# A DiT block on one core: transposing bf16 activations on TensorE as 4-byte pairs of neighbouring values

## The chip, the cores and the metric

The kernel is one block of a diffusion transformer (DiT) and runs on one core of one Trainium2 chip. The metric is the device time of one execution in microseconds (us), the median of several runs. Most runs of one kernel on one chip lie within about 0.3% of each other.

Names used below: PE is TensorE's matmul stream and PEld its weight loads, DVE is VectorE, ACT is ScalarE, POOL is GpSimd. SBUF is the on-chip memory that holds the operands, PSUM the one that matmuls write to. A "k-tile" is one of the 9 pieces of 128 features into which the model width of 1152 is cut. LN1 and LN2 are the two LayerNorms.

## The reference, cut to what matters

```python
B, N, D = 2, 256, 1152            # 512 tokens in 4 tiles of 128; 9 k-tiles
shift_a, scale_a, gate_a, shift_m, scale_m, gate_m = ...   # silu(c) @ w_mod
h = layernorm(x) * (1 + scale_a) + shift_a
q, k, v = (h @ wqkv) ...                                   # 2 heads of 576
attn = softmax(q @ k.T * Dh ** -0.5)
x = x + gate_a * ((attn @ v) @ wo)
h2 = layernorm(x) * (1 + scale_m) + shift_m
out = x + gate_m * (gelu(h2 @ w_fc1) @ w_fc2)              # width 4 * D
```

The kernel's matmuls contract over partitions (the 128 rows of the on-chip memories). So the outputs of LN1, softmax and LN2, which have tokens on partitions, must be transposed before the next matmul. The kernel does it on TensorE: the data is the stationary operand, an identity is the moving one, the result lands in PSUM, and VectorE or ScalarE carries it on to SBUF, applying the LayerNorm's scale on the way.

## The kernel before: the parts that matter

LN1. `ps16(bank, c, n)` is a bf16 view of a PSUM bank; there are 8 banks.

```python
XB = [(4, 5, 6), (6, 4, 5)]
def xn_T(t):                      # 9 transposes for each token tile
    b = t // 2
    for kt in range(KT):
        tr(ps16(XB[b][kt // 4], (kt % 4) * 256 + (t % 2) * 128, 128), XN[:, t, kt * 128:(kt + 1) * 128], IDENT)
# ... cut: k-tiles 0 to 4 are scaled from PSUM (hk), k-tiles 5 to 8 are copied (xnT_cp)
for kt in range(KC):
    hk(kt, 0, "act" if kt in (2, 4) else "dve")
```

LN2: k-tiles 0 to 3 go to bank 7 and 4 to 8 to bank 6. In the first two token tiles VectorE scales 0 to 3 and ScalarE 4 to 8.

```python
def xn2_T(t):
    slot = [ps16(7, kt * 128, 128) if kt < 4 else ps16(6, (kt - 4) * 128, 128) for kt in range(KT)]
    for kt in range(KT):
        tr(slot[kt], xn2[:, kt * 128:(kt + 1) * 128], IDENT)
    for kt in range(KT):
        if kt < (4 if t < 2 else 6):
            dve(335, lambda ...: e.tensor_scalar(out=dst, in0=o, scalar1=s1, scalar2=s2, ...), ..., "h2T_%d_%d" % (t, kt))
        else:
            act(440, lambda ...: e.activation(out=dst, in_=o, func=ACTF.Identity, scale=s1, bias=s2), ..., "h2T_%d_%d" % (t, kt))
```

The kernel schedules itself: a list scheduler puts the units of work of VectorE and ScalarE in an order, from dependences that a tracker records. The tracker's rule for PSUM:

```python
for b in reg.banks():
    if eng == "pe":
        # ... cut: a PE write waits for every earlier reader of the whole bank
    else:
        for u in self.bank_pe[b]:
            self._add_dep(ins, u.instrs[-1])       # a reader waits for the last transpose of the tile that wrote to the bank
        for o in self.bank_other[b]:
            if o.unit.eng != eng:
                self._add_dep(ins, o)              # and for each earlier reader of the bank on ANOTHER engine
            # ... cut: readers on the same engine
```

The rule is needed. The Trainium skill, "PSUM — Partial Sum Buffer", section "PSUM bank collisions raise a hardware error", says that no two of TensorE, ScalarE and VectorE may be in one bank and 32-partition quadrant at once, reads against reads included, and that software has to keep them apart.

Of the kernel before, what the change touches and what calls it, by code (L numbers as in the profile page):

```python
# [492 lines left out]
BF16 = mybir.dt.bfloat16  # L493
F32 = mybir.dt.float32
ALU = mybir.AluOpType
ACTF = mybir.ActivationFunctionType
AX = mybir.AxisListType

P = 128
NTOK = 512  # L500
D = 1152
KT = 9
# [5 lines left out]
CH = 384  # L508
NCH = 3
F0 = 8  # L510
KC = 5
# [3 lines left out]
def c_mm(n):  # L515
    return max(n / 2.4 + 2.5, 27.0)
# [26 lines left out]
def build_kernel(nc, x, c, wqkv, wo, w_mod, w_fc1, w_fc2, out):  # L543
    S = Sched()
# [4 lines left out]
    with (  # L549
        nc.sbuf_tensor("arena", [P, ARENA_BYTES // 2], BF16) as arena,  # L550
        nc.psum_tensor("psum", [P, 4096], F32) as psum,
        nc.Block() as block,
    ):
        def sb(off, nbytes, dt=BF16):
            assert off % 4 == 0 and off + nbytes <= ARENA_BYTES, (off, nbytes)
            v = arena[:, off // 2:(off + nbytes) // 2]
            if dt == F32:
                v = v.bitcast(F32)
            return v
# [22 lines left out]
        def misc(nbytes):  # L582
            o = mo[0]
            mo[0] += (nbytes + 3) // 4 * 4
            assert mo[0] <= ARENA_BYTES
            return o
# [36 lines left out]
        IDENT = sb(misc(256), 256)  # L623
        ONES = sb(misc(256), 256)
        CSB = sb(misc(256), 256)
        TH = sb(misc(72), 72, F32)
# [23 lines left out]
        outv = out.rearrange("b (p t) d -> b p t d", t=2)  # L650
        wqkv_v = wqkv.rearrange("(k p) f -> p k f", p=P)
        wmod_v = w_mod.rearrange("(k p) f -> p k f", p=P)
        wo_v = wo.rearrange("(k p) f -> p k f", p=P)
        wfc1_v = w_fc1.rearrange("(k p) f -> p k f", p=P)
        wfc2_v = w_fc2.rearrange("(k p) f -> p k f", p=P)

        def dma(dst, src, nbytes, name, is_out=False, eng="sp", run=4096):
            eff = 1.0 if run >= 4096 else (1.08 if run >= 2304 else (1.15 if run >= 1536 else (1.3 if run >= 1024 else 1.42)))
            return S.op(eng, 500.0 if eng == "sp" else 150.0, lambda e: e.dma_start(dst, src), reads=[src], writes=[dst],  # L659
                        name=name, dma_bytes=nbytes * eff, is_out=is_out)  # L660

        def dve(cost, fn, reads, writes, name):
# [14 lines left out]
        def mm(o, l, r, st, sp, **kw):  # L677
            S.instr(lambda e: e.matmul(o, lhsT=l, rhs=r, start=st, stop=sp, **kw), reads=[l, r], writes=[o])  # L678

        def tr(o, i_, idn):  # L680
            S.instr(lambda e: e.transpose(o, i_, idn), reads=[i_, idn], writes=[o])  # L681
# [5 lines left out]
        for (ka, kb) in ((0, KC), (KC, KT)):  # L687
            w = (kb - ka) * P
            for k0 in range(0, KT, 3):
                dma(WSC[:, k0:k0 + 3, ka * P:kb * P], wmod_v[:, k0:k0 + 3, D + ka * P:D + kb * P], 3 * P * w * 2,  # L690
                    "ld_sc%d_%d" % (ka, k0), run=w * 2)
            for kt in range(ka, kb):
                dma(WK[:, kt, :], wqkv_v[:, kt, D:2 * D], P * D * 2, "ld_wk%d" % kt, run=2304)
        for k0 in range(0, KT, 3):
            dma(WSH[:, k0:k0 + 3, :], wmod_v[:, k0:k0 + 3, 0:D], 3 * P * D * 2, "ld_sh%d" % k0, run=2304)

        def wfc1_load(q):
            dma(WFC1[q % 4], wfc1_v[:, :, q * 512:(q + 1) * 512], D * 512 * 2, "ld_wfc1_%d" % q, run=1024)

# [3 lines left out]
             reads=[ONES], writes=[IDENT], name="ident")  # L703

        S.op("pool", 100, lambda e: e.memset(NHALF, -0.5), writes=[NHALF], name="nhalf")

# [44 lines left out]
        def xn_T(t):  # L751
            b = t // 2
            S.unit("pe", KT * c_mm(128), "xnT_%d" % t)
            for kt in range(KT):
                tr(ps16(XB[b][kt // 4], (kt % 4) * 256 + (t % 2) * 128, 128), XN[:, t, kt * 128:(kt + 1) * 128], IDENT)

        def xn_T_copy(b, k0, k1, eng):
            src = ps16(XB[b][k0 // 4], (k0 % 4) * 256, (k1 - k0) * 256).rearrange("p (k t) -> p k t", k=k1 - k0)
            copy_on(eng, HX[:, k0:k1, b * 256:(b + 1) * 256], src, (k1 - k0) * 256, True, "xnT_cp%d_%d" % (b, k0))

# [5 lines left out]
        def mod_kt(W, kt, col0, name, fs=(0, 9)):  # L766
            S.unit("pe", (fs[1] - fs[0]) * 27.0, name)
            for f in range(*fs):
                mm(ps32(7, col0 + f * 2, 2), W[:, kt, f * 128:(f + 1) * 128], ST[:, kt:18:9], kt == 0 and f == fs[0], kt == KT - 1,
                   skip_group_check=True)  # L770
# [6 lines left out]
        def hk(kt, b, eng="dve"):  # L777
            dst, s1 = HK[:, kt, b * 256:(b + 1) * 256], SC1A[:, kt * 2 + b:kt * 2 + b + 1]
            src = ps16(XB[b][kt // 4], (kt % 4) * 256, 256) if kt < KC else HX[:, kt, b * 256:(b + 1) * 256]
            if eng == "act":  # L780
                act(c_act(256, 1), lambda e: e.activation(out=dst, in_=src, func=ACTF.Copy, scale=s1), [src, s1], [dst], "hk_%d_%d" % (kt, b))
                return
            dve(256 if kt < KC else 200, lambda e: e.tensor_scalar(out=dst, in0=src, scalar1=s1, scalar2=None, op0=ALU.mult),  # L783
                [src, s1], [dst], "hk_%d_%d" % (kt, b))
# [38 lines left out]
        for kt in range(KC):  # L823
            hk(kt, 0, "act" if kt in (2, 4) else "dve")
        xn_T_copy(0, 8, 9, "act")
        xn_T_copy(0, 5, 8, "act")
        for kt in range(KC):
            for i in range(4):
                k_pair((kt,), i, 0)
            if kt == 1:  # L830
                xn_T(2)
            if kt == 2:
                xn_T(3)
                xn_T_copy(1, 8, 9, "act")
                xn_T_copy(1, 5, 8, "act")
        for kt in range(KC):
# [10 lines left out]
        for kt in range(KT):  # L847
            dma(WQ[:, kt, :], wqkv_v[:, kt, 0:D], P * D * 2, "ld_wq%d" % kt, run=2304)
        for kt in range(KC, KT - 2):
# [25 lines left out]
        for kt in range(KT):  # L875
            mod_kt(WSH, kt, 18, "sh_%d" % kt)
        dma(WV, wqkv_v[:, :, 2 * D:3 * D], D * D * 2, "ld_wv", run=2304)
        for k0 in range(0, KT, 3):
# [3 lines left out]
        for kt in range(KT):  # L882
            for b in range(2):
# [5 lines left out]
                else:  # L889
# [9 lines left out]
                    "sc1a_0", "hk_0_0", "xn_2", "hk_1_0", "xn_3", "hk_3_0", "z4a", "hk_0_1", "hk_1_1", "hk_3_1", "hk_4_1", "sc1a_5"],  # L899
            "act": ["ld_c", "c_tanh", "sq_ln1_0", "sum_ln1_0", "sq_ln1_3", "sum_ln1_3", "xnT_cp0_8", "xnT_cp0_5", "hk_2_0", "hk_4_0",  # L900
                    "hk_2_1", "xnT_cp1_8", "xnT_cp1_5"],
        }
# [27 lines left out]
        def pt_transposes(b, h):  # L930
            idx = b * 2 + h
            bank = s_bank[(b, h)]
            S.unit("pe", 4 * c_mm(128), "PT_%d_%d" % (b, h))
            for kjt in range(2):
                for jq in range(2):
                    tr(ps16(bank, kjt * 256 + jq * 128, 128), PP[idx][:, jq, kjt * 128:(kjt + 1) * 128], IDENT)
            copy_on("dve" if b == 0 else "act", PTS[idx].rearrange("p j k -> p (j k)"), ps16(bank, 0, 512), 512, True, "PT_ev%d" % idx)

# [3 lines left out]
        def v_proj(t, ci):  # L942
            bank = v_banks[v_rr[0] % 3]
            v_rr[0] += 1
            S.unit("pe", KT * c_mm(CH), "v_%d_%d" % (t, ci))
            o = ps32(bank, 0, CH)
            for kt in range(KT):
                mm(o, HX[:, kt, t * 128:(t + 1) * 128], WV[:, kt, ci * CH:(ci + 1) * CH], kt == 0, kt == KT - 1)
            copy_on("act" if v_rr[0] % 2 else "dve", V[:, t, ci * CH:(ci + 1) * CH], o, CH, False, "v_ev%d_%d" % (t, ci))
# [23 lines left out]
        def rows_T():  # L973
            for j, bank in ((0, 3), (1, 4)):
                S.unit("pe", 9 * 30.0 + 100.0, "rowsT%d" % j)
                for r in range(3):
                    for i3 in range(3):
                        ft = r * 3 + i3
                        tr(ps16(bank, ft * 2, 2), ROWS[32 * j:32 * j + 2, r, i3 * 128:(i3 + 1) * 128], IDENT[32 * j:32 * j + 2, 32 * j:32 * j + 2])
            a, b_ = ps16(3, 0, 18), ps16(4, 0, 18)  # L980
            dve(170, lambda e: e.tensor_copy(SHM, a), [a], [SHM], "shm")
            dve(170, lambda e: e.tensor_scalar(out=SC1M, in0=b_, scalar1=1.0, scalar2=None, op0=ALU.add), [b_], [SC1M], "sc1m")
# [52 lines left out]
        def xn2_T(t):  # L1035
            b = t // 2
            xn2 = XN2[t]
            S.unit("pe", KT * c_mm(128), "xn2T_%d" % t)
            slot = [ps16(7, kt * 128, 128) if kt < 4 else ps16(6, (kt - 4) * 128, 128) for kt in range(KT)]
            for kt in range(KT):  # L1040
                tr(slot[kt], xn2[:, kt * 128:(kt + 1) * 128], IDENT)
            for kt in range(KT):
# [153 lines left out]
```

## Time and profile before

| | before |
|---|---|
| time, median of 4 runs | 249.73 us (249.42 to 249.81) |
| profiled span | 247.4 us |
| PE busy | 241.7 us, 98% |
| first K matmul to the second-half modulation matmuls (LN1 stretch) | 6.66 us |
| from there to the first LN2 transpose | 78.30 us |
| first LN2 transpose to the end of the fourth LN2 tile (LN2 stretch) | 12.62 us |
| first LN2 transpose to the last matmul | 147.38 us |

The last four rows are differences of matmul start times in the trace (of the last matmul, its end). Since PE is busy nearly all the time, such a table of PE's own milestones says which stage a change moved.

From the profile page of the kernel before: the span, PE's row, and the chain of waits that ended last, by engine.

```profile
span 247.4 us, 4146 instructions
...
PE 241.7 (98%) x1827; PEld 149.5 (60%) x1827; DVE 69.9 (28%) x179; ACT 63.8 (26%) x129; POOL 19.6 (8%) x33
...
PE 94%; ACT 2%; DMA 2%; DVE 1%; issue 0%
```

PE bounds the kernel. Before, from its groups of instructions by line (L681 is the transpose helper, L1049 and L1046 are the LN2 scalings, L783 the LN1 scalings). The columns are busy us and mean ns of one, then idle time before and what ended it:

```profile
L681 PE MATMUL psum<-arena 128*128 128x128 bf16 (+2 forms) x107 | 7.8, 209 | 0.9 <-DMA arena<-in_c_dram 0.7
L1049 ACT ACTIVATE arena<-psum,arena 128x128 bf16<-128x128 bf16 x16 | 6.1, 460 | 3.2 <-PE psum L681 2.5
L1046 DVE TENSOR_SCALAR arena<-psum,arena 128x128 bf16<-128x128 bf16 x20 | 5.5, 338 | 2.0 <-PE psum L681 1.8
L783 DVE TENSOR_SCALAR arena<-psum,arena 128x256 bf16<-128x256 bf16 x7 | 2.4, 349 | 2.7 <-PE psum L681 1.4
```

The 209 ns is the length of one record; records overlap. Successive transposes start 55.9 ns apart, and that spacing is what they cost PE.

Before, timeline of the first LN2 tile's scalings and the second tile's transposes (start us, us, engine, line, count, idle before):

```profile
97.68 1.16 ACT L1049 ACTIVATE arena<-psum,arena 128x128 bf16<-128x128 bf16 x3 [1.94 <-PE psum L681]
97.68 0.60 DVE L1046 TENSOR_SCALAR arena<-psum,arena 128x128 bf16<-128x128 bf16 x2
...
98.78 1.35 ACT L1033 ACTIVATE arena<-arena 128x1152 bf16<-128x1152 f32 x1
...
100.03 0.79 ACT L1049 ACTIVATE arena<-psum,arena 128x128 bf16<-128x128 bf16 x2
...
100.24 0.37 PEld L681 LDWEIGHTS psum<-arena 128*128 128x128 bf16 x4
...
100.87 0.28 PEld L681 LDWEIGHTS psum<-arena 128*128 128x128 bf16 x5 [0.26 <-ACT arena L1049]
```

ScalarE does three scalings, then the next tile's normalisation (L1033, 1.35 us), then its last two, ending at about 100.82. Meanwhile PE does the second tile's first four transposes, into bank 7, which VectorE has left. Only the five for bank 6 wait, 0.26 us of idle weight load. (Elsewhere in this text a gap on PE is the time between two matmul starts beyond their usual spacing, which comes to 0.25 us here; the brackets in the views give idle time, which is often shorter.)

### The profile page before, as it was taken

What the parts mean: (1) busy time and instruction counts of PE and PEld (TensorE: products, weight loads), DVE (VectorE), ACT (ScalarE), POOL (GpSimd) and SP (SyncE); (2) the same over time, 40 slices, a digit from 0 to 9 for tenths busy, and PEclk for the clock granted to TensorE, in tenths of its full rate; (3) what the DMA queues carried; (4) which work ended last, traced back from release to release, by engine and by line L of the source; (5) the groups of instructions that cost most, each with busy time, mean ns of one, the idle gap of its engine ahead of it and who ended that gap; (6) DMA issues with size and microseconds to landing.
All of it is one profiled execution on the core that took longest, in us unless ns stands there. A gap on an engine that the chain in (4) does not pass through costs nothing.

```text
span 247.4 us, 4146 instructions
## 1 busy us (share of the span) xinstructions
PE 241.7 (98%) x1827; PEld 149.5 (60%) x1827; DVE 69.9 (28%) x179; ACT 63.8 (26%) x129; POOL 19.6 (8%) x33
## 2 busy tenths in 40 slices
PE   6999999999999999999999999999999999999995
PEld 2589954566656766798544444444566666666674
DVE  3742440555322679950000000000012222111112
ACT  4730340344301404984333222332000000000000
POOL 1300000000013167500000000000000000000000
PEclk9999999999999999999999999999999999999999
DMA  6999989999999999999953660000000000000000
GB/s 240 372 375 393 390 299 414 426 423 420 409 385 332 309 364 391 392 386 383 358 156 138 191 191 3 0 0 0 3 16 16 19 16 16 16 19 21 27 19 17
DMA packets 27644, 51.59 MB, mean 209 GB/s; under 512 B 1511, under 2 KB 15591, under 8 KB 26475
## 3 DMA queue, kind: packets, MB, share of 16 engines
q1 hardware_dynamic: 27216, 50.14, 56.0%
q0 software_dynamic: 384, 1.19, 1.5%
q8 instruction: 14, 0.23, 0.4%
q14 instruction: 3, 0.02, 0.0%
q10 hardware_dynamic: 27, 0.00, 0.0%
HBM read 50.14 MB, written 1.19 MB: 208 GB/s over the span
## 4 chain that ended last, share of the span: by engine, by line
PE 94%; ACT 2%; DMA 2%; DVE 1%; issue 0%
PE psum L678 92%; PE psum L681 2%; DMA arena<-in_x_dram 2%; ACT arena L1049 1%; ACT arena L1033 1%; ACT arena L731 1%; ACT arena L730 1%; DVE arena L744 0%; DVE arena L783 0%; DVE arena L1139 0%; DVE arena L732 0%; DVE arena L1140 0%; DVE arena L774 0%; DVE arena L734 0%
## 5 line engine op out<-in xcount | busy, mean ns | idle before, releaser
L678 PE MATMUL psum<-arena 128*128 128x384 bf16 (+7 forms) x1720 | 237.7, 305 | 1.8 <-POOL arena L701 1.4
L678 PEld LDWEIGHTS psum<-arena 128*128 128x128 bf16 (+1 forms) x1720 | 143.8, 97 | 91.0 <-issue 3.1
L1139 DVE TENSOR_TENSOR arena<-psum,arena 128x384 f32<-128x384 f32 (+3 forms) x14 | 7.0, 501 | 119.2 <-PE psum L678 119.2
L1059 ACT ACTIVATE arena<-psum 128x512 bf16<-128x512 f32 (+1 forms) x44 | 22.5, 522 | 42.6 <-PE psum L678 42.6
L673 ACT ACTIVATE arena<-psum 128x512 bf16<-128x512 f32 (+7 forms) x29 | 15.4, 553 | 36.2 <-PE psum L678 33.8
L675 DVE CAST arena<-psum 128x512 bf16<-128x512 f32 (+4 forms) x23 | 14.0, 621 | 32.1 <-PE psum L678 32.0
L1028 POOL TENSOR_TENSOR arena<-arena 128x384 f32<-128x384 f32 x12 | 11.0, 913 | 11.2 <-DVE arena L1027 10.0
L722 DVE BATCH_NORM_STATS2 arena<-arena 128x6 f32<-128x384 f32 (+1 forms) x18 | 9.5, 548 | 0.8 <-DMA arena<-in_x_dram 0.7
L681 PE MATMUL psum<-arena 128*128 128x128 bf16 (+2 forms) x107 | 7.8, 209 | 0.9 <-DMA arena<-in_c_dram 0.7
L681 PEld LDWEIGHTS psum<-arena 128*128 128x128 bf16 (+2 forms) x107 | 6.3, 97 | 3.7 <-DMA arena<-in_c_dram 1.6
L1033 ACT ACTIVATE arena<-arena 128x1152 bf16<-128x1152 f32 x4 | 5.4, 1353 | 9.5 <-DVE arena L1032 9.5
L1027 DVE TENSOR_TENSOR arena<-psum,arena 128x384 f32<-128x384 f32 x12 | 6.6, 548 | 3.2 <-PE psum L678 2.6
L1140 DVE TENSOR_TENSOR arena<-arena 128x384 bf16<-128x384 f32 (+3 forms) x14 | 7.0, 501 | 0.5
L1049 ACT ACTIVATE arena<-psum,arena 128x128 bf16<-128x128 bf16 x16 | 6.1, 460 | 3.2 <-PE psum L681 2.5
L659 POOL DMA_DIRECT2D dit_scratch<-arena x2 | 1.2, 629 | 61.3 <-DVE arena L675 61.3
L1046 DVE TENSOR_SCALAR arena<-psum,arena 128x128 bf16<-128x128 bf16 x20 | 5.5, 338 | 2.0 <-PE psum L681 1.8
L924 ACT ACTIVATE arena<-psum,arena 128x256 bf16<-128x256 f32 x8 | 3.7, 471 | 6.9 <-PE psum L678 5.4
L726 POOL TENSOR_TENSOR arena<-arena 128x1 f32<-128x1 f32 x6 | 3.3, 553 | 8.7 <-DVE arena L725 8.7
L887 ACT ACTIVATE arena<-arena 128x256 bf16<-128x256 bf16 x6 | 2.5, 496 | 4.3 <-DVE arena L881 4.3
L920 DVE TENSOR_REDUCE arena<-psum 128x2 f32<-128x512 f32 x4 | 2.8, 690 | 1.5 <-PE psum L678 1.5
L783 DVE TENSOR_SCALAR arena<-psum,arena 128x256 bf16<-128x256 bf16 x7 | 2.4, 349 | 2.7 <-PE psum L681 1.4
L928 DVE TENSOR_TENSOR arena<-arena 128x512 bf16<-128x512 bf16 x4 | 2.8, 688 | 0.1
(37 smaller groups left out, 30.9 us busy)
## 6 DMA issues: line engine op xcount, KB each, us to landing
arena<-in_w_mod_dram SPq DMA_DIRECT2D x3, 3456.0 KB, 25.9
arena<-in_w_fc_dram SPq DMA_DIRECT2D x9, 1152.0 KB, 8.6
arena<-in_w_fc_dram SPq DMA_DIRECT2D x4, 2592.0 KB, 20.7
arena<-in_wqkv_dram SPq DMA_DIRECT2D x18, 288.0 KB, 10.0
arena<-in_w_mod_dram SPq DMA_DIRECT2D x3, 864.0 KB, 13.1
arena<-in_wqkv_dram SPq DMA_DIRECT2D x1, 2592.0 KB, 10.0
arena<-in_wo_dram SPq DMA_DIRECT2D x1, 2592.0 KB, 39.7
arena<-in_w_mod_dram SPq DMA_DIRECT2D x3, 480.0 KB, 6.8
```

Source lines behind the costliest of these rows:

```text
L673: act(c_act(n), lambda e: e.activation(out=dst, in_=src, func=ACTF.Copy), [src], [dst], name)
L675: dve(c_dve_psum16(n) if psum16 else c_dve_psum32(n), lambda e: e.tensor_copy(dst, src), [src], [dst], name)
L678: S.instr(lambda e: e.matmul(o, lhsT=l, rhs=r, start=st, stop=sp, **kw), reads=[l, r], writes=[o])
L681: S.instr(lambda e: e.transpose(o, i_, idn), reads=[i_, idn], writes=[o])
L722: dve(550, lambda e, s=s, o=o: e.bn_stats(out=o, in_=s), [s], [o], "bn_%s_%d" % (tag, ci))
L1027: dve(550, lambda e, o=o, ga=ga, x1c=x1c: e.tensor_tensor(out=x1c, in0=o, in1=ga, op=ALU.mult), [o, ga], [x1c], "wo_t1_%d_%d" % (t, ci))
L1028: S.op("pool", 930, lambda e, xs=xs, x1c=x1c: e.tensor_tensor(out=x1c, in0=x1c, in1=xs, op=ALU.add), reads=[x1c, xs], writes=[x1c], name=" ...
L1033: act(1344, lambda e: e.activation(out=xn2, in_=x1, func=ACTF.Identity, scale=rs, bias=nm), [x1, rs, nm], [xn2], "xn2_%d" % t)
L1049: act(440, lambda e, o=o, dst=dst, s1=s1, s2=s2: e.activation(out=dst, in_=o, func=ACTF.Identity, scale=s1, bias=s2), [o, s1, s2], [dst], ...
L1059: act(c_act(ntok), lambda e: e.activation(out=dst, in_=o, func=ACTF.Gelu_apprx_tanh), [o], [dst], "gelu_%d_%d" % (f, tok0))
L1139: dve(c_dve_psum32(w), lambda e, o=o, gm=gm, t1=t1: e.tensor_tensor(out=t1, in0=o, in1=gm, op=ALU.mult), [o, gm], [t1], "fc2_t1_%d_%d" % ( ...
L1140: dve(c_dve_32(w), lambda e, t1=t1, x1c=x1c, ost=ost: e.tensor_tensor(out=ost, in0=t1, in1=x1c, op=ALU.add), [t1, x1c], [ost], "fc2_out_%d ...
```

## The change

A 128x256 block of bf16 is a 128x128 block of 4-byte words, each holding two neighbouring features. One 4-byte transpose then does the work of two: row p of the result holds features 2p and 2p+1 of the pair of k-tiles, alternating. Since 9 is odd, the first 128 features keep a 2-byte transpose of their own. The rest follows from the interleaving: weight rows are loaded in a permuted order to match, the engines that empty PSUM read every second bf16, and modulation columns and V tokens are taken with a step of two. The intent is fewer PE instructions, 5 transposes for 9 in each LayerNorm tile and 2 for 4 in each softmax tile. Core of the diff, cuts marked:

```diff
+        def tr4(o, i_):
+            o4, w0 = o.bitcast(F32R), int(i_.offset) % (ARENA_BYTES // 2) // 2
+            S.instr(lambda e: e.transpose(o4, words[:, w0:w0 + P], IDENT4W), reads=[i_, IDENT4], writes=[o])
 # ... cut: weight loads with permuted rows, fcols() = every second column
         def xn_T(t):
             b = t // 2
-            for kt in range(KT):
-                tr(ps16(XB[b][kt // 4], (kt % 4) * 256 + (t % 2) * 128, 128), XN[:, t, kt * 128:(kt + 1) * 128], IDENT)
+            tr(ps16(XB[b][2], (t % 2) * 128, 128), XN[:, t, 0:P], IDENT)
+            for g in range(4):
+                tr4(ps32(XB[b][g // 2], (g % 2) * 256 + (t % 2) * 128, 128), XN[:, t, P + 256 * g:P + 256 * (g + 1)])
 # ... cut: xn_src() = every second bf16 of PSUM; one copy of 1024 elements for two of 256 and 768
         def pt_transposes(b, h):
-            for kjt in range(2):
-                for jq in range(2):
-                    tr(ps16(bank, kjt * 256 + jq * 128, 128), PP[idx][:, jq, kjt * 128:(kjt + 1) * 128], IDENT)
+            for jq in range(2):
+                tr4(ps32(bank, jq * 128, 128), PP[idx][:, jq, :])
 # ... cut: V tokens with a step of two
         def xn2_T(t):
-            slot = [ps16(7, kt * 128, 128) if kt < 4 else ps16(6, (kt - 4) * 128, 128) for kt in range(KT)]
-            for kt in range(KT):
-                tr(slot[kt], xn2[:, kt * 128:(kt + 1) * 128], IDENT)
+            slot = [ps16(6, 512, 128)]
+            tr(slot[0], xn2[:, 0:P], IDENT)
+            for g in range(4):
+                bank, c0 = (7, g * 128) if g < 2 else (6, (g - 2) * 128)
+                tr4(ps32(bank, c0, 128), xn2[:, P + 256 * g:P + 256 * (g + 1)])
+                v = ps16(bank, 2 * c0, 256).rearrange("p (t i) -> p i t", i=2)
+                slot += [v[:, 0, :], v[:, 1, :]]
```

In LN2 each 4-byte result holds a pair of k-tiles, so bank 7 now holds k-tiles 1 to 4 and bank 6 holds 5 to 8 and, behind them, k-tile 0. The split of work between the engines (VectorE 0 to 3, ScalarE 4 to 8) is left as it was.

## The prediction

> **What bounds the kernel.** The profile page has PE busy for 241.7 of 247.4 us; the chain of waits lies on PE for 94% of the span, and from 15.8 us on it leaves PE only at the second-LayerNorm (LN2) transposes (97.7 to 100.8 us, ScalarE) and at the end. Starts in the trace are even: 128x512 matmuls every 215.8 ns, 384 every 162.5, 256 every 109.2, two-column modulation matmuls every 26.7, transposes every 55.9. PE time removed is time saved, unless something else is just behind PE.
>
> **What the change does on PE.** 88 transposes cost 88 x 55.9 = 4.92 us. After: 8 bf16 ones and 40 four-byte ones, each still one weight load and one matmul. No trace here times a four-byte one; call it p. The PE change is 40p - 80 x 55.9 ns: -2.2 us at p = 56, zero at p = 112. The data is the stationary operand. The Trainium skill, "TensorE: Matmul & The Clock Gate", "Weight-path perf modes", excludes FP32 from fast weight load, and its "LDWEIGHTS" section gives columns / 1.2, so 107 ns for 128. I expect the load to set p: 70 to 115 ns, central estimate 90, and PE work to fall by about 0.9 us.
>
> **What stands just behind PE.**
> - LN1: the second-half modulation weights land at 19.05 us; the matmuls needing them start at about 19.3. At most 0.3 us of LN1's saving can show. The new placement puts k-tiles 1 to 4 in one bank, used alternately by VectorE and ScalarE: the third tile's transposes wait for ScalarE's scaling of k-tile 4, 0.3 to 0.6 us of new stall near 14 us. It also separates ScalarE's copy from k-tile 4, removing two stalls before 18.5 us (0.06, 0.13 us). Net 0 to 0.2 us gained.
> - Softmax: four tiles on the chain: 4 x (224 - 2p), 0.2 us gained.
> - LN2: 4 x (503 - 56 - 4p), 0.35 us gross, but the second tile already waits for ScalarE (0.25 us) and arriving earlier only lengthens that. Net 0 to 0.2.
>
> **Added work elsewhere.** VectorE reads every second bf16 of PSUM. 512-element copies took 424 ns (bf16) and 690 ns (fp32), so I estimate half rate for strided reads: +133 ns on a 256-element scaling (349 to about 480), +67 on a 128-element one (338 to about 405), +266 on softmax copies. Mostly off the chain; perhaps 0.2 us of waiting in LN2. ScalarE: one 1024-element copy near 1.05 us replaces 384 + 805 ns. Modulation and V weight loads now step by two elements; I expect the 26.7 ns pace to hold. If it doubled, 144 loads would cost 3.8 us: the largest risk. Weight bytes and run lengths are unchanged; 20 more DMA issues should not be felt.
>
> **Prediction.** 249.3 us, 8 in 10 between 247.9 and 251.8. Faster by over 2%: 2%; within 2%: 92%; slower by over 2%: 6%.
>
> **What would show it.** Four-byte transposes starting 70 to 115 ns apart; strided VectorE scalings near 480 and 405 ns; a gap inside the third LN1 tile near 14 us waiting for ScalarE; two-column matmuls still 26.7 ns apart; second-half modulation matmuls beginning at most 0.3 us earlier; LN2 gaps of 0.2 to 0.6 us at the second or fourth tile.
>
> **What would make it wrong.** p near 56 with no new LN2 waits: about 248.5. p of 160 or more (load and matmul not overlapping): 251 to 253. Strided weight loads slower than the 26.7 ns pace: up to 4 us worse. Strided reads stalling the first feed-forward tiles by over 0.5 us.

## More of the kernel before

Before, windows of the trace (start:end, length, then busy us of each engine), for the LN1 stretch, what lies between, and the LN2 stretch:

```profile
core 0: us, PE busy (x) PEld busy (x) DVE busy (x) ACT busy (x) POOL busy (x), PEclk, DMA share, GB/s
12.02:18.68 6.66, 6.66 (x68) 5.74 (x69) 3.11 (x9) 2.29 (x5) 0.00 (x0) 1.00 1.08 377
18.68:96.98 78.30, 78.30 (x715) 51.08 (x713) 34.74 (x85) 21.01 (x48) 11.00 (x15) 1.00 1.02 381
96.98:109.60 12.62, 12.53 (x118) 9.93 (x117) 9.84 (x30) 11.34 (x23) 5.47 (x8) 1.00 1.05 392
```

In the LN2 stretch ScalarE is busy 11.3 of 12.6 us and VectorE 9.8: these two have little slack there.

## The result, and the profile after

The kernel after took 250.69 us (median of 4 runs, 250.44 to 250.94) against 249.73 before in the same rounds. The ratio is 1.0042, 95% interval 1.0027 to 1.0056: "the same" at 2%, but a small loss for certain. A ratio here is the mean time of one kernel's fast runs over the mean of the other's in the same rounds, so it is not quite the ratio of the medians quoted beside it.

Work was taken off PE, as the page shows, and yet the span grew:

```profile
span 249.1 us, 4079 instructions
...
PE 240.2 (96%) x1777; PEld 148.3 (60%) x1787; DVE 71.5 (29%) x179; ACT 63.8 (26%) x127; POOL 19.9 (8%) x34
...
PE 91%; DMA 3%; DVE 2%; ACT 1%; SPq 1%; issue 1%
```

After, groups by line (L705 is the 4-byte transpose; L1091, L1088 and L822 answer to L1049, L1046 and L783):

```profile
L1091 ACT ACTIVATE arena<-psum,arena 128x128 bf16<-128x128 bf16 x16 | 6.1, 461 | 4.8 <-PE psum L701 4.8
L1088 DVE TENSOR_SCALAR arena<-psum,arena 128x128 bf16<-128x128 bf16 x20 | 6.5, 390 | 2.5 <-PE psum L705 2.5
...
L705 PE MATMUL psum<-ident,words 128*128 128x128 f32 x40 | 6.0, 261 | 0.4 <-DVE arena L909 0.4
...
L822 DVE TENSOR_SCALAR arena<-psum,arena 128x256 bf16<-128x256 bf16 x7 | 2.9, 443 | 2.4 <-PE psum L705 1.7
```

The means of L1088 and L822 mix strided reads with the plain reads of k-tile 0. Strided alone they take about 402 ns (338 before) and 475 to 484 ns (349 before). ScalarE's take 461 (460): no cost there.

After, windows for the same three stretches:

```profile
core 0: us, PE busy (x) PEld busy (x) DVE busy (x) ACT busy (x) POOL busy (x), PEclk, DMA share, GB/s
...
12.41:19.21 6.80, 6.43 (x61) 5.66 (x62) 3.68 (x9) 2.34 (x4) 0.00 (x0) 1.00 1.08 378
19.21:97.17 77.96, 77.78 (x703) 50.89 (x704) 35.28 (x85) 21.02 (x48) 10.99 (x15) 1.00 1.03 383
97.17:111.30 14.13, 12.47 (x103) 9.27 (x100) 10.01 (x30) 11.47 (x23) 5.47 (x8) 1.00 1.03 385
```

| stage, in PE's milestones | before | after | difference |
|---|---|---|---|
| start to the first K matmul | 12.02 | 12.41 | +0.39 |
| LN1 stretch | 6.66 | 6.80 | +0.14 |
| up to LN2 (softmax lies here) | 78.30 | 77.97 | -0.33 |
| first LN2 transpose to the last matmul | 147.38 | 148.90 | +1.52 |
| sum, to the last matmul | 244.36 | 246.07 | +1.71 |

The first row looks like chance: the first K matmul waits for modulation weights, and over all 13 traces of whole kernels it starts between 11.66 and 12.54 us with no relation to the form of LN1 (two-byte LN1: 12.02, 12.05, 12.35, 12.39, 12.54; four-byte: 11.66 to 12.54). Without it the trace has +1.33 us, and the timed runs +0.96. So the stage sums are good to some 0.4 us, and the story is the last row: LN2 lost 1.5 us.

After, the timeline that answers to the one of before:

```profile
97.85 0.66 DVE L1088 TENSOR_SCALAR arena<-psum,arena 128x128 bf16<-128x128 bf16 x2
...
98.28 0.81 ACT L1091 ACTIVATE arena<-psum,arena 128x128 bf16<-128x128 bf16 x2 [2.35 <-PE psum L701]
...
98.86 0.72 DVE L1088 TENSOR_SCALAR arena<-psum,arena 128x128 bf16<-128x128 bf16 x2
98.98 1.34 ACT L1071 ACTIVATE arena<-arena 128x1152 bf16<-128x1152 f32 x1
...
100.23 1.14 ACT L1091 ACTIVATE arena<-psum,arena 128x128 bf16<-128x128 bf16 x3
...
101.48 0.10 PEld L708 LDWEIGHTS psum<-arena 128*128 128x128 bf16 x1 [1.22 <-DVE arena L754]
101.51 0.22 PE L708 MATMUL psum<-arena 128*128 128x128 bf16 x1 [0.86 <-DVE arena L1065]
```

ScalarE no longer starts together with VectorE. VectorE's first scaling, k-tile 0 in bank 6, runs from 97.85 to 98.18; ScalarE's semaphore event passes at 98.22 and its first scaling, in the same bank, starts at 98.28. The same is seen in the second tile (VectorE's k-tile 0 ends at 102.79, ScalarE starts at 102.89). Having started late, ScalarE fits only two scalings ahead of the normalisation, so three remain and the last ends at 101.37 (before: 100.82). And since k-tile 0's transpose, the first of the tile, goes into bank 6, the whole second tile waits for it: PE's semaphore event is at 101.41 and the weight load at 101.48.

The bracket names VectorE's L1065 as the releaser, the multiplication of a later tile's attention output by its gate. It neither writes what the transposes read nor reads their banks; it merely ended at about the same time. The PE gap is 1.03 us long. Two more follow: 0.64 us in all inside the first feed-forward tile (0.10 us until VectorE's k-tile 3 is scaled, then 0.54 us until k-tile 4 is, which lies in VectorE's bank 7 and which the scheduler now puts fourth of ScalarE's five), and 0.60 us before the fourth tile's transposes. Before, LN2's gaps summed to 0.31 us. So the waits grew by 1.96 us while four tiles saved 4 x 0.12 = 0.47 us.

Near 14 us, in the third LN1 tile, the stall that was predicted from the same rule (L820 is ScalarE's scaling of k-tile 4, L909 an idle-time memset):

```profile
14.20 0.34 PE L705 MATMUL psum<-ident,words 128*128 128x128 f32 x2
14.29 0.47 ACT L820 ACTIVATE arena<-psum,arena 128x256 bf16<-128x256 bf16 x1 [0.55 <-DVE arena L822]
...
14.88 0.14 PEld L705 LDWEIGHTS psum<-ident,words 128*128 128x128 f32 x1 [0.48 <-DVE arena L909]
```

PE stops after two 4-byte transposes, until ScalarE has left the bank: about 0.53 us. Here too the bracket names an innocent instruction.

### The profile page after: what moved, and what is told of

It is laid out like the page before. It is cut to its first block, busy times and chain, and to the rows that moved or that the text cites. A ratio compares the mean times of both kernels' runs of the same rounds, so it can differ in the third digit from the quotient of the medians.

```text
span 249.1 us, 4079 instructions
## 1 busy us (share of the span) xinstructions
PE 240.2 (96%) x1777; PEld 148.3 (60%) x1787; DVE 71.5 (29%) x179; ACT 63.8 (26%) x127; POOL 19.9 (8%) x34
## 4 chain that ended last, share of the span: by engine, by line
PE 91%; DMA 3%; DVE 2%; ACT 1%; SPq 1%; issue 1%
PE psum L701 90%; DMA arena<-in_w_mod_dram 3%; ACT arena L1091 1%; PE psum L705 1%; SPq L666 1%; DVE arena L1065 1%; DVE arena L1088 0%; PE psum L708 0%; DVE arena L753 0%; DVE arena L1070 0%; ACT arena L1101 0%; DVE arena L822 0%; DVE arena L909 0%; DVE arena L1181 0%; DVE arena L1182 0%
## 5 line engine op out<-in xcount | busy, mean ns | idle before, releaser
L1101 ACT ACTIVATE arena<-psum 128x512 bf16<-128x512 f32 (+1 forms) x44 | 22.5, 522 | 42.6 <-PE psum L701 42.6
L696 ACT ACTIVATE arena<-psum 128x512 bf16<-128x512 f32 (+6 forms) x27 | 15.3, 582 | 35.5 <-PE psum L701 33.4
L1065 DVE TENSOR_TENSOR arena<-psum,arena 128x384 f32<-128x384 f32 x12 | 6.6, 548 | 3.2 <-PE psum L701 3.0
L1091 ACT ACTIVATE arena<-psum,arena 128x128 bf16<-128x128 bf16 x16 | 6.1, 461 | 4.8 <-PE psum L701 4.8
L1088 DVE TENSOR_SCALAR arena<-psum,arena 128x128 bf16<-128x128 bf16 x20 | 6.5, 390 | 2.5 <-PE psum L705 2.5
L705 PE MATMUL psum<-ident,words 128*128 128x128 f32 x40 | 6.0, 261 | 0.4 <-DVE arena L909 0.4
L705 PEld LDWEIGHTS psum<-ident,words 128*128 128x128 f32 x40 | 4.4, 141 | 0.9 <-DVE arena L909 0.5
L708 PE MATMUL psum<-arena 2*128 2x2 bf16 (+2 forms) x27 | 2.5, 179 | 2.5 <-DVE arena L1065 0.9
L708 PEld LDWEIGHTS psum<-arena 2*128 2x128 bf16 (+2 forms) x27 | 1.3, 93 | 5.0 <-DMA arena<-in_c_dram 1.7
L822 DVE TENSOR_SCALAR arena<-psum,arena 128x256 bf16<-128x256 bf16 x7 | 2.9, 443 | 2.4 <-PE psum L705 1.7
```

What stands on the lines that cost most here:

```text
L696: act(c_act(n), lambda e: e.activation(out=dst, in_=src, func=ACTF.Copy), [src], [dst], name)
L705: S.instr(lambda e: e.transpose(o4, words[:, w0:w0 + P], IDENT4W), reads=[i_, IDENT4], writes=[o])
L1065: dve(550, lambda e, o=o, ga=ga, x1c=x1c: e.tensor_tensor(out=x1c, in0=o, in1=ga, op=ALU.mult), [o, ga], [x1c], "wo_t1_%d_%d" % (t, ci))
L1088: dve(335, lambda e, o=o, dst=dst, s1=s1, s2=s2: e.tensor_scalar(out=dst, in0=o, scalar1=s1, scalar2=s2, op0=ALU.mult, op1=ALU.add), [o, s ...
L1091: act(440, lambda e, o=o, dst=dst, s1=s1, s2=s2: e.activation(out=dst, in_=o, func=ACTF.Identity, scale=s1, bias=s2), [o, s1, s2], [dst], ...
L1101: act(c_act(ntok), lambda e: e.activation(out=dst, in_=o, func=ACTF.Gelu_apprx_tanh), [o], [dst], "gelu_%d_%d" % (f, tok0))
```

## The experiments

The main theory: LN2's new PSUM places make two engines take turns in one bank, and this alone is the loss. Rivals: the slower strided reads of VectorE; the LN1 stall; a higher cost of 4-byte transposes in context; another order of work that the scheduler picked. Twelve runs were made of eleven kernels, in four groups: experiments 1 to 4; 5, 6, 7 and 8; 9, h1_all_banks and g1_again; and h2_act_order. Each group has runs of the kernel before on its own chip (experiment 8 was run once, for its trace only). Groups 1 and 2 ran on the same chip.

### 1. LN2 put back, the rest of the change kept (e1_ln2_bf16)

```diff
-            slot = [ps16(6, 512, 128)]
-            # ... one two-byte and four 4-byte transposes
+            slot = [ps16(7, kt * 128, 128) if kt < 4 else ps16(6, (kt - 4) * 128, 128) for kt in range(KT)]
+            for kt in range(KT):
+                tr(slot[kt], xn2[:, fcols(kt)], IDENT)
```

> The changed kernel with only its LN2 transposes put back to two-byte ones in the old PSUM places (weights stay permuted; the transposes read every second column). Theory A (the loss is the new PSUM placement in LN2: k-tile 0 lies in the bank that ScalarE drains, k-tile 4 in VectorE's, so engines and the next tile's transposes wait): in the changed kernel's trace LN2 lost 1.5 us against before, so about 249.2 us here, 0.2 to 0.8 us below the kernel before, and the gaps of 1.03, 0.54 and 0.60 us on PE between 100 and 111 us go back to the 0.25 and 0.06 us of before. Rival B (the loss is in LN1 or in later weights): about 250.5 us and the LN2 gaps unchanged in size.

Measured: 248.99 us, ratio 0.9974 (0.9959 to 0.9989), now faster than before. LN2's gaps are those of the kernel before and the LN2 stretch is 12.62 us. So the loss sits in LN2's part of the change.

### 2. LN1 put back, the rest kept (e3_ln1_plain)

```diff
-            tr(ps16(XB[b][2], (t % 2) * 128, 128), XN[:, t, 0:P], IDENT)
-            # ... 4-byte transposes, strided sources, permuted weight rows
+            for kt in range(KT):
+                tr(ps16(XB[b][kt // 4], (kt % 4) * 256 + (t % 2) * 128, 128), XN[:, t, kt * 128:(kt + 1) * 128], IDENT)
```

> The changed kernel with LN1 wholly as before (two-byte transposes, old PSUM places, unpermuted rows of the qkv and modulation weights); softmax and LN2 four-byte. In the changed kernel's trace the first 60 us lost 0.5 us, of which 0.4 came before the first K matmul because a modulation weight landed 0.76 us later. Theory D (that lateness is chance or belongs to one trace, the LN1 part itself is worth nothing): within 0.2 us of the changed kernel, 250.5 to 250.8. Rival E (LN1's part costs 0.5 us in every run): 250.2 us, and the weight lands at 10.3 us again.

Measured: 250.77 us, ratio 1.0043 (1.0029 to 1.0056), the same as the kernel after (1.0042). The LN1 stretch is 6.66 us, as before, against 6.80. The LN1 part is worth nothing measurable as written: its transposes are cheaper and its stall takes that back.

### 3. The kernel before, with LN2's PSUM places alone changed (f1_before_banks)

```diff
-            slot = [ps16(7, kt * 128, 128) if kt < 4 else ps16(6, (kt - 4) * 128, 128) for kt in range(KT)]
+            slot = [ps16(6, 512, 128) if kt == 0 else ps16(7, (kt - 1) * 128, 128) if kt < 5 else ps16(6, (kt - 5) * 128, 128) for kt in range(KT)]
```

No 4-byte transpose and no strided read is in this kernel; only addresses in PSUM differ.

> The kernel before with nothing changed but the LN2 PSUM places: k-tile 0 in the bank of k-tiles 5 to 8, k-tiles 1 to 4 in the other. No four-byte transpose and no strided read. Theory A: it loses most of what LN2 lost, plus 0.8 to 1.6 us (250.5 to 251.3). Rival C (strided reads are what makes LN2 late): within 0.2 us of the kernel before.

Measured: 251.19 us, ratio 1.0070 (1.0045 to 1.0094). One of its six runs stands apart (252.98 us, at a clock of 0.993); without it the ratio of the means is 1.0058. From the first LN2 transpose to the last matmul it takes 148.85 us (before 147.38, after 148.90). Its timeline shows the mechanism bare:

```profile
98.05 0.59 DVE L1046 TENSOR_SCALAR arena<-psum,arena 128x128 bf16<-128x128 bf16 x2
...
98.49 0.81 ACT L1049 ACTIVATE arena<-psum,arena 128x128 bf16<-128x128 bf16 x2 [2.39 <-DVE arena L1046]
...
99.19 1.34 ACT L1033 ACTIVATE arena<-arena 128x1152 bf16<-128x1152 f32 x1
...
100.43 1.15 ACT L1049 ACTIVATE arena<-psum,arena 128x128 bf16<-128x128 bf16 x3
...
101.69 0.41 PEld L681 LDWEIGHTS psum<-arena 128*128 128x128 bf16 x7 [1.14 <-DVE arena L725]
```

VectorE at 98.05, ScalarE only at 98.49 and this time with VectorE's L1046 named as the releaser; two scalings ahead of the normalisation and three behind it; the second tile 0.95 us late. Gaps of 0.36 us (k-tile 4 in the first feed-forward tile) and 0.50 us (before the fourth tile) follow. So the places alone, without any of the change's arithmetic, are enough for the loss: strided reads and dear transposes are not needed for it. They may still have a part in the rest: the kernel after has 0.5 us more of gaps than this one (0.10 us at VectorE's k-tile 3, which this kernel does not wait for, and 0.18, 0.08 and 0.11 us more at the three gaps that both have), and no run separates the causes of these.

### 4. k-tile 0 moved to the other bank (e2_ln2_banks)

```diff
-            slot = [ps16(6, 512, 128)]
+            slot = [ps16(7, 512, 128)]
-                if kt < (4 if t < 2 else 6):
+                if kt < 5:
```

Now VectorE has bank 7 (k-tiles 0 to 4) and ScalarE bank 6 (5 to 8), in every tile.

> The changed kernel with four-byte transposes kept in LN2, but k-tile 0 moved into the bank of k-tiles 1 to 4, all of these for VectorE, and the other bank (k-tiles 5 to 8) for ScalarE alone. Theory A (sharing of a bank by two engines): the three LN2 gaps shrink to under 0.3 us each; 249.0 to 249.4 us. Rival C (VectorE's slower strided reads, 402 instead of 338 ns, make LN2 late): VectorE has one more such read per tile in the first two tiles, so the gaps stay and the time is 250.5 us or more.

Measured: 250.37 us, ratio 1.0029 (1.0014 to 1.0043): a miss. The gap at the second tile shrank from 1.03 to about 0.05 us and the one in the first feed-forward tile went, as expected. But the scheduler, with five scalings on VectorE, put the third token tile's statistics behind them (their aggregation at 102.35 us, 100.56 before), and PE waited 0.82 us for the third tile's normalisation and 0.80 us before the fourth tile. Separate banks are not enough where the two engines have little slack: the order of work counts as well.

### 5. Banks by engine, and the order fixed by hand (g2_ln2_order)

```diff
+            n7 = 1 if t == 1 else 2        # how many pairs go to bank 7
-                if kt < (4 if t < 2 else 6):
+                if kt < (5, 3, 7, 7)[t]:
+        for names in (LN2_DVE, LN2_ACT):   # two lists that give the order on VectorE and ScalarE
+            us = [next(u for u in S.units if u.name == n) for n in names.split()]
+            for u0, u1 in zip(us, us[1:]):
+                S.order_after(u1, u0)
```

> The changed kernel, all three places four-byte, with LN2's banks split by engine (tile by tile: 5/4, 3/6, and for the last two tiles five k-tiles alone in VectorE's bank, ScalarE only two) and with the order of work on VectorE and ScalarE between 97 and 112 us fixed by hand, so that the third token tile's statistics come before the second tile's scalings. Theory A': e2's two remaining gaps (0.82 and 0.80 us) came from that order, not from four-byte transposes: the gaps fall under 0.3 us each, the LN2 stretch (first LN2 transpose to the end of the fourth tile) from 13.64 us in e2 to 12.0 to 12.6, the time to 248.6 to 249.3 us. Rival F (VectorE and ScalarE have no room for the strided reads in this stretch): it stays above 13 us and the time above 249.7.

Measured: 249.60 us, ratio 0.9995 (0.9982 to 1.0008), which misses the range given for the time. The LN2 stretch is 12.78 us, just above what was expected, since one gap of 0.64 us stayed: the fourth tile's second half waits for VectorE's last evictions of the third tile in bank 6. So 1.2 us of the 1.5 us lost in LN2 came back by places, order and the split of the work (VectorE has 22 scalings here, 20 in the kernel after), with strided reads and 4-byte transposes kept. Bank 6 still has two readers in the last two tiles.

### 6. Banks by engine in LN1, on top of experiment 1 (g1_ln1_banks, and again as g1_again)

```diff
-        XB = [(4, 5, 6), (6, 4, 5)]
+        XB = [(4, 5), (6, 4)]      # k-tiles 0 to 2 in a bank for VectorE, 3 to 8 in banks for ScalarE
-            hk(kt, 0, "act" if kt in (2, 4) else "dve")
+            hk(kt, 0, "act" if kt in (3, 4) else "dve")
```

> The e1 kernel (LN2 back to two-byte transposes; LN1 and softmax four-byte) with LN1's PSUM places changed: k-tiles 0 to 2 in a bank that only VectorE scales from, k-tiles 3 and 4 and the copied ones in banks that only ScalarE reads. Theory A (two engines taking turns in one bank, and the next tile waiting for the last turn, cost 0.53 us in the third LN1 tile): the gap inside the third tile goes, the stretch from the first K matmul to the second-half modulation matmuls falls from 6.80 us to about 6.2, and the time to 248.4 to 248.8 us, 0.3 to 0.5 us under e1's. Rival: the modulation weights, which landed between 17.8 and 19.1 us in the traces so far, take the gain back: as e1, about 249.0.

> g1_ln1_banks again, for a comparison with h1_all_banks on one chip in the same rounds: 248.4 to 248.8 us, 0.4% under before.

The split and the order change with the places (cut above): of the second 256 tokens ScalarE now scales k-tiles 3 and 4 and VectorE k-tile 2, and ScalarE's copy comes before its scalings.

Measured: 248.57 us, ratio 0.9956 (0.9942 to 0.9970), and on another chip 248.95 us, 0.9975 (0.9961 to 0.9988); the second median lies just above the range given for it. The stall near 14 us is gone and the LN1 stretch is 6.27 us (before 6.66, after 6.80). The same transposes that were worth nothing are worth 0.39 us of this stretch, in both traces, when no bank is shared. The times alone show it less surely: the first is 0.18 points under experiment 1's ratio, the second the same as it (0.9974).

### 7. The softmax part alone (g3_pt_only)

The kernel before, with the diff's `pt_transposes` and V tokens only.

> The kernel before with the softmax part of the change alone (two four-byte transposes per tile, V's tokens taken in steps of two). In the changed kernel's trace each of the four tiles took 1.602 us with its V matmuls in place of 1.686: minus 0.34 us, so 249.2 us. A strided V weight load that is slower would show as V matmuls more than 162.5 ns apart; none was seen.

Measured: 249.33 us, ratio 0.9986 (0.9971 to 1.0000). A softmax transpose tile with the V matmuls around it went from 1.69 to 1.60 us, four of them -0.34 us. Here both 4-byte results have one bank and one reader, and the saving shows in full. It also times a 4-byte transpose in that context: two cost 4 x 55.9 - 84 = 140 ns, so 70 ns each.

### 8. The disputed costs by themselves (m1_costs)

The kernel after, with bursts of transposes put between the feed-forward matmuls, whose results are thrown away.

> The changed kernel with bursts of transposes added before the last matmuls (output unchanged; about 11 us longer). Spacing of starts, 24 each: two-byte dense 55.9 ns; two-byte with every second column 55.9 ns; four-byte 128x128 86 to 88 ns. If the weight load sets that pace, four-byte with 64 moving columns (data on 64 partitions) stays at 85 ns and with 64 stationary columns falls to about 55; if the moving side sets it, the other way round. A lone four-byte transpose between 384-column matmuls: about 60 to 70 ns added, as in the softmax part, because its load hides behind the matmul before it; a lone two-byte one 56.

Measured, as start-to-start time on PE (one look; the bursts took 22 us and the run 272.54 us, more than was allowed for):

| burst | ns each |
|---|---|
| 2-byte 128x128, plain or every second column | 55.8 |
| 4-byte 128x128 | 87.0 |
| 4-byte, 64 moving columns | 84 |
| 4-byte, 64 stationary columns | about 60 |
| a single 2-byte one between 384-column matmuls | 56 |
| a single 4-byte one between 384-column matmuls | about 77 |

The last row is worked out: four wide matmuls and one 4-byte transpose take 0.526 + 0.201 us, the four alone 0.650; it lies above the 60 to 70 ns expected. Halving the moving columns (and with them the partitions of the data) takes off under 3 ns and halving the stationary ones takes off 27 ns: the weight load sets the pace, as the prediction had it. A rival in which 4-byte transposes cost more than two 2-byte ones falls: 87 against 112 ns.

### 9. The shared places, with the order of the kernel before (f2_places_order)

Experiment 3 left open whether the bank or the scheduler's reaction to it costs the time.

```diff
+        for names in (LN2_DVE, LN2_ACT):   # the order that VectorE and ScalarE had in the kernel before
+            us = [next(u for u in S.units if u.name == n) for n in names.split()]
+            for u0, u1 in zip(us, us[1:]):
+                S.order_after(u1, u0)
```

> The kernel before, two-byte transposes everywhere, with only LN2's PSUM places changed as in f1_before_banks, but with the order of LN2's work on VectorE and ScalarE held to that of the kernel before. f1 cost 0.7%. Theory A1 (the shared bank itself costs: a tile's transposes wait for two engines' evictions, whatever the order): the loss stays, time 250.3 to 251.5, first to fourth LN2 tile 13.6 to 14.5 us long on PE, a gap of 0.7 us or more before the second tile's transposes. Rival A2 (the loss in f1 was only the other order that the scheduler chose because of the places): time within 0.3 us of before (249.3 to 249.9), the stretch 12.6 to 12.9 us. A time between 249.9 and 250.3 says that both have a part.

Measured: 253.71 us, ratio 1.0165 (1.0151 to 1.0180), LN2 stretch 16.03 us. The rival falls, and the first theory's own number was far too small.

```profile
98.21 0.59 DVE L1048 TENSOR_SCALAR arena<-psum,arena 128x128 bf16<-128x128 bf16 x2
...
99.19 0.58 DVE L1048 TENSOR_SCALAR arena<-psum,arena 128x128 bf16<-128x128 bf16 x2
...
99.87 1.15 ACT L1051 ACTIVATE arena<-psum,arena 128x128 bf16<-128x128 bf16 x3 [3.61 <-PE psum L680]
...
103.10 0.27 PE L683 MATMUL psum<-arena 128*128 128x128 bf16 x2 [2.01 <-ACT arena L1051]
```

The old order has ScalarE begin with k-tile 4, in bank 7. It must wait for VectorE's k-tiles 1 to 3, which end at 99.78; ScalarE starts at 99.87, 2.37 us after the tile's first transpose (0.70 us in the kernel before), and PE then waits 2.01 us in one piece (a gap of 2.17 us). In the kernel after and in experiment 3, whose orders in LN2 are the same when the two kernels are built, the scheduler had put k-tile 4 behind two of bank 6 in the first tile and behind three in the second, and so had avoided the worse half of this.

Two readers need not cost much where the order suits them: in the kernel before, bank 6 has two in the last two tiles, VectorE takes k-tiles 4 and 5 first, and PE waits 0.06 us there.

### 10. All banks by engine (h1_all_banks), and one order mended (h2_act_order)

The LN1 banks of experiment 6 with the LN2 of experiment 5 (bank 6 keeps its two readers in the third tile), and the fourth tile's second half in bank 1, taken from the feed-forward accumulators, so that it need not wait for the third tile's readers:

```diff
-                bank, c0 = (7, g * 128) if g < n7 else (6, (g - n7) * 128)
+                bank, c0 = (7, g * 128) if g < n7 else (1 if t == 3 else 6, (g - n7) * 128)
-                if kt < (5, 3, 7, 7)[t]:
+                if kt < (5, 3, 7, 5)[t]:
```

> The whole change with PSUM places by engine in LN1 (as g1) and in LN2 (as g2), and the fourth LN2 tile's second half given a bank of its own, so that it need not wait for VectorE's last evictions of the third tile. If the last 0.64 us gap of g2 was a matter of places: that gap goes, the LN2 stretch is 12.0 to 12.4 us and the time 248.0 to 248.5, under g1 of the same rounds by 0.2 to 0.6 us. Rival (no room left on VectorE and ScalarE with the slower strided evictions, so a wait comes up elsewhere): stretch 12.6 or more, time within 0.3 us of g1 or above it; then four-byte transposes in LN2 are worth nothing even with good places.

Measured: 249.15 us, ratio 0.9982 (0.9970 to 0.9995): a miss, and no better than g1_again in the same rounds. The LN2 stretch is 12.11 us, as expected, but then PE waited 0.84 us behind it. The timeline of h1 (L1101 is ScalarE's LN2 scaling, L1111 the GELU):

```profile
109.79 0.66 ACT L1111 ACTIVATE arena<-psum 128x256 bf16<-128x256 f32 x2 [0.74 <-PE psum L706]
110.33 0.46 ACT L1101 ACTIVATE arena<-psum,arena 128x128 bf16<-128x128 bf16 x1
...
111.05 1.15 ACT L1101 ACTIVATE arena<-psum,arena 128x128 bf16<-128x128 bf16 x3
111.56 0.10 PEld L706 LDWEIGHTS psum<-arena 128*128 128x128 bf16 x1 [0.45 <-ACT arena L1101]
```

ScalarE sat idle for 0.74 us waiting for a GELU's matmuls while the fourth tile's scalings were ready. So the rival (no room on the engines) was not shown; the order was at fault. One edit puts the four scalings ahead of two GELUs:

```diff
-... gelu_4_0 gelu_5_0 h2T_3_5 h2T_3_6 h2T_3_7 h2T_3_8
+... gelu_4_0 gelu_5_0 h2T_3_5 h2T_3_6 h2T_3_7 h2T_3_8 gelu_6_0 gelu_7_0
```

> h1_all_banks with one change of order on ScalarE: the fourth LN2 tile's four scalings go ahead of the GELU evictions of the feed-forward tiles 6 and 7, which in h1 stood among them and waited for PE. In h1 the LN2 stretch was short (12.1 us) but PE then waited 0.84 us for these scalings, so the 0.5 us gained was given back. If that order alone is the cause: the waits after the fourth tile go, first LN2 transpose to last matmul is 146.8 to 147.0 us (before 147.4, h1 147.7), and the time is about 0.8 us under h1's ratio, so 0.994 to 0.996 of before (248.2 to 248.8 us). Rival (ScalarE or VectorE is simply full there with the strided reads): a wait of 0.4 us or more comes up elsewhere and the ratio stays at 0.997 or above.

Measured: 248.39 us (248.22 to 248.71), ratio 0.9941 (0.9928 to 0.9955), the fastest of all. From the first LN2 transpose to the last matmul it takes 146.89 us (before 147.38, h1 147.70), inside what was expected. The whole change with places and order to suit: LN1 -0.39, softmax -0.33, LN2 -0.49 us by the milestones, together -1.21 us (the times say -1.3 us by the medians, -1.5 us by the ratio).

### What could not be tried

The wait itself cannot be taken away alone. A version of the kernel after, without the tracker's rule between two readers, builds and is refused by the race check, with VectorE and ScalarE reading bank 7 unordered; it was not run.

## Why the prediction was right or wrong, point by point

- **Total.** 249.3 us was predicted with a range of 247.9 to 251.8; 250.69 was measured. The class and the range held, the sign did not: a gain of 0.4 us was foretold and there was a loss of 1.0 us. That the range held is in part luck: its upper end was there for slow strided weight loads or a p of 160 ns, and neither came.
- **PE bounds the kernel.** Right. Every stage's gap on PE reappears in the span, and the stage sums of all variants agree with their times to about 0.4 us (0.6 in experiment 9, where two of the four runs were at a clock of 0.991 and 0.993).
- **Pace of a 4-byte transpose, 70 to 115 ns, centre 90, set by the weight load.** Right: 87 to 90 ns on average in a LayerNorm tile, 70 in the softmax context, 87.0 in bursts, and the stationary columns set it. The Trainium skill, "TensorE: Matmul & The Clock Gate", section "LDWEIGHTS", would give 107 ns for 128 columns; the trace has 20 ns less.
- **Work taken off PE, about 0.9 us.** Somewhat small: eight LayerNorm tiles went from 0.503 to 0.385 us (-0.94) and the softmax tiles gave -0.34, so 1.28 us. The best version realises 1.21 us of it.
- **VectorE's strided reads at half rate: 480, 405 and 690 ns.** Right: 475 to 484, about 402 and 692 ns. The Trainium skill, "VectorE: DVE Perf Modes", section "Mode 2×_1P — pack two bf16 into one 32-bit read", has the reason: two bf16 per read need a step of one. The trace agrees with that: a softmax copy of 512 went from 424 to 692 ns, which is what 512 fp32 values from PSUM take here too (690). ScalarE's single copy took 1.02 us (1.05 foretold).
- **Modulation loads keep their 26.7 ns pace.** Right, and V matmuls kept 162.5 ns. The largest feared risk did not come.
- **LN1: a stall of 0.3 to 0.6 us near 14 us, net 0 to 0.2 us gained.** The stall was right in place, cause and size (0.53 us), and the two old ones went. The net was nothing: the stretch grew by 0.14 us, and putting LN1 back changed the time by nothing.
- **Softmax: 0.2 us gained.** Right in kind, 0.33 us in size: a 4-byte transpose cost 70 ns there and not the 90 put into the sum.
- **LN2: "Net 0 to 0.2" gained, with "perhaps 0.2 us of waiting".** This is the step that failed. It measured 1.52 us lost: 0.47 us gained by cheaper transposes against 1.96 us more waiting. The prediction named the places where waits would rise (second and fourth tile), but sized them at 0.2 to 0.6 us together with an old wait that "arriving earlier only lengthens". The cause in LN2 was the rule it had just applied to LN1, two engines in one bank, but it never laid LN2's k-tiles over the banks. Doing so would have shown that ScalarE cannot start before VectorE's k-tile 0 is done, and that the first transpose of a tile needs ScalarE's bank. Experiment 3 shows that this alone costs 1.47 us; experiments 5 and 10 show that it can be had back.
- **What would make it wrong: "strided reads stalling the first feed-forward tiles by over 0.5 us".** The first feed-forward tile was stalled by 0.64 us in all, but 0.54 us of it for k-tile 4's turn on ScalarE, whose own reads are no slower, and only 0.10 us for a strided read of VectorE; with banks by engine and strided reads kept it went (experiment 4).

What stays open: how the kernel after's 0.5 us of waiting beyond experiment 3 divides between strided reads and the earlier arrival of PE; why experiment 1's time fell by more (0.65 us) than its stages explain (0.2 us); and how much of the start to the first K matmul is chance.

## What to carry to other kernels

When a change moves results in PSUM, draw the map of banks against the engines that read them, for every place where it applies: two readers in one bank run one after the other, and the next tile's transposes into it wait for the later of the two. What that costs is a matter of order and slack: 0.06 us in the kernel before, 1.5 us in experiment 3. On the engine that bounds a kernel, cheaper instructions show only if what releases them comes no later; here 1.3 us of saved transposes became 1.0 us of loss through addresses, and a gain of about 1.4 us through other addresses, another split of the work and orders to suit. Where the profile names a releaser, check that the named instruction really writes or reads something the waiting one needs.

## What the Trainium skill lacked or had wrong

- "TensorE: Matmul & The Clock Gate", "LDWEIGHTS": 107 ns for 128 columns by its rule; transposes with 4-byte loads here start 87 to 90 ns apart for 128 columns and about 60 ns for 64, and alone between wide matmuls cost 77 ns or less; the record of one such load is 141 ns long (97 for 2-byte).
- The same page, "Part 4: PE-mode transpose": it gives about 275 to 390 ns for a transpose. One record is 219 ns (2-byte) or 261 ns (4-byte) long here; in a row they start 55.9 ns apart (2-byte) or 87 ns (4-byte). The page has nothing on transposing bf16 as 4-byte pairs.
- The same page, "Back-to-back issue gap": about 81 ns sustained for 128 columns and 131 ns for 512 with a weight load for each matmul; this case has 55.9 and 215.8 ns, both with a load for each, which is what the section's formula for isolated matmuls gives (about 56 and 216 ns).
- "VectorE: DVE Perf Modes" gives the condition on the step, and 120 + elements / (elements per cycle) cycles at 0.96 GHz from PSUM to SBUF. An estimate from that is 192 and 258 ns (128 elements, step of one and of two), 258 and 392 (256), 392 and 658 (512); measured were 338 and 402, 349 and 480, 424 and 692. What the step adds agrees; the whole is too low, most of all for the short scalings. For ScalarE no page says that the step costs nothing there: 460 to 461 ns.
- "PSUM — Partial Sum Buffer", "PSUM bank collisions raise a hardware error": it gives the rule but not what obeying it can cost: +0.7% of the whole kernel from addresses alone (experiment 3), +1.65% with an order that does not allow for it (experiment 9).
